# q and k of six head groups turned in 32x32 blocks on VectorE, with permuted products, in a routed attention and gated convolution kernel

## The chip, the core and the metric

The kernel runs on one core of one Trainium2 chip. A core has TensorE (PE: matmuls, and transposes done as matmuls against an identity), VectorE (DVE), ScalarE (ACT), GpSimd (POOL) and SyncE (SP, which here only issues DMAs). The metric is device time in microseconds of one execution; a profile is one further execution with the hardware profiler on.

## The reference, cut to what matters

```python
# q, k, v: [4, 8, 768, 64] f32; centroids: [8, 16, 64]
q_assign = argmax(q_n @ c_n^T)              # nearest of 16 centroids, per query (q_n, c_n: normalised)
k_assign = argmax(k_n @ c_n^T)              # the same per key
scores = where(q_assign == k_assign, (q @ k^T) / 8, -1e9)
attn = exp(scores - max(scores)); attn = attn / (sum(attn) + 1e-9)
x = attn @ v                                # heads side by side: [4, 768, 512]

proj = x @ w_proj                           # [.., 1536] -> x1, x2, x3 of 512
y = x1 * irfft(rfft(x2) * rfft(filter)) * x3     # circular convolution along the 768 rows
out = y @ w_out                             # [4, 768, 512] f32
```

## The kernel before

The 32 heads (4 batches of 8) are worked in eight *groups* of four heads, n = 0 to 7, and each group in two *pairs* of heads, pr = 0 and 1. Two groups make a batch. For each group the steps are:

- **Loads** (`load_qk`, `load_v`, on SP's queue). A q or k tile `qkraw` holds a pair's 768 rows as 128 partitions x 6 rows x 2 heads x 64 numbers; there are four such buffers (`NQK`), so all are used once per group. Each tile comes in two DMAs, one per head, with rows of 64 f32 (256 bytes). v (`vraw`, three buffers) comes in one DMA per pair.
- **Turning q and k** (`routing`). The scores need q and k with the 64 head dimensions on the partitions. For groups 2 to 7, `tr2` (line 594) makes 12 TensorE transposes of 128x128 per pair into three PSUM banks, six of q and six of k; three copies (the helper `copy`, lines 282 and 284) bring them by ACT or DVE to `qkP` in SBUF. Groups 0 and 1 use single banks (line 607).
- **Routing masks** (`routing`, continued). Centroid products by TensorE (line 627), a 32x32 block transpose of the result on DVE (line 632), a maximum, a comparison (lines 638, 640), a second block transpose (line 642), and eight small DMAs (line 497) put the one-hot rows under q and k in the `aug` tiles, where a large constant makes a mask of them. The `aug` tiles take q and k as bf16 casts from `qkP` (by ACT, DVE or POOL).
- **Attention** (`attention`). For each of six key tiles: scores by TensorE (helper `product`, line 84), exponentials by ACT (lines 694, 697) into one of five f32 buffers `p`, the product with v on TensorE in f32 (line 708), and the row sums, accumulated element by element in `acc`: the first two tiles are added in three 512-wide pieces (line 725, DVE or POOL), the other four in one 1536-wide addition each (line 729, DVE). After the sixth tile, ACT copies the result from PSUM to `osb` (line 732). `acc` is reduced across partitions by accumulating DMAs issued on POOL (line 762) and small DMAs on SP, or, in the first two groups and the last, by a matmul; the reciprocals are spread to `rb` (two DMAs to 64 partitions), and one DVE instruction (line 808) computes `(osb + eps) * rb` into the bf16 tile `xT`. `eps` is a column that the v product yields beside its 768 results.
- **Gated convolution** (`hyena`), once per batch: projections of `xT` (line 843), spectrum, product with the filter (line 873), inverse (line 84), folds (lines 944, 954), gates `x1 * x3` (line 917), the product with them (line 959), and the output projection.

The order of the work is not written by hand: every step is an operation with a duration, a set of engines that may run it, and a due time; a planner (`Plan.place`) puts them on the engines one by one, and the program is issued in that order. The tables `NUDGE` (a correction to the due time of each operation, by its number) and `ONLY` (a fixed engine for some) go into it. Each engine then runs its instructions in its order, and waits on semaphores where data or a buffer is not ready. Operations marked `lock` are those with SBUF operands on DVE and POOL; a POOL one of them is made to wait for the last DVE one ahead of it.

Of the kernel before, what the change touches and what calls it, by code (L numbers as in the profile page):

```python
# [18 lines left out]
Act = mybir.ActivationFunctionType  # L19
# [13 lines left out]
NV = 3  # L33
NU = 4
ROWS = 16
LEAD = 0.0
# [228 lines left out]
def build(T):  # L265
# [31 lines left out]
    def two(h):  # L297
        return T.pair[2]
# [16 lines left out]
    def load_qk(n, pr, j, due, after=()):  # L315
        s = qslot[n, pr, j] = len(loads) % NQK
        loads.append(1)

        src = lambda: (T.q, T.k)[j][n // 2, 4 * (n % 2) + 2 * pr:4 * (n % 2) + 2 * pr + 2].rearrange("h (p t) d -> p t h d", t=NT)
        for x in range(2):  # L320
            for half in ((0,), (1,)) if n == pr == 0 else ((0, 1),):
                t = slice(3 * half[0], 3 * half[-1] + 3)
                op({"SP": .66, "ACT": .66} if n == 0 else ("SP", .66), lambda e, x=x, t=t: dma(e)(
                    T.qkraw[s][:, t, x], src()[:, t, x]), due, w=[("qkraw", s, x, c) for c in half],
                   byts=98e3 * len(half), kind="load", after=after, lat=.3 if n else -.5)

    def load_v(n, pr, due, after=()):
        op(("SP", .6), lambda e: T.nc.sync.dma_start(
            T.vraw[(2 * n + pr) % NV], T.v[n // 2, 4 * (n % 2) + 2 * pr:4 * (n % 2) + 2 * pr + 2].rearrange(
                "h (p t) d -> p h (t d)", t=NT)), due, w=[("vraw", (2 * n + pr) % NV)], byts=LOAD, kind="load",  # L330
           after=after)
# [242 lines left out]
    def routing(n):  # L574
# [5 lines left out]
        for u in range(8):  # L580
# [7 lines left out]
            if n > 1 and z % 2 == 0 and ch == 0:  # L588
                h = Bank(cls, 3)
                ss = [qslot[n, pr, x] for x in range(2)]  # L590

                def tr2(e, ss=ss, h=h):
                    for i in range(2 * NT):
                        T.nc.tensor.transpose(bank(h.ids[i // 4])[:, ts(i % 4, 128)], raw(ss[i // NT], i % NT), T.ident[:, ::-1] if 3 <= i < NT else T.ident)  # L594
                op(("PE", 1.42), tr2, due, r=[("qkraw", s, x, c) for s in ss for x in range(2) for c in range(2)] + ["ident"], w=[h], alloc=h)
                for c in range(3):
                    op(EV512, lambda e, pr=pr, c=c, h=h: copy(e, T.qkP[pr][:, ts(c, 512)], bank(h.ids[c])), due + 1.6,
                       r=[h], w=[("qkT", 2 * pr + x, y) for x, y in ((0, 0), (0, 1), (0, 2), (1, 0), (1, 1), (1, 2))[2 * c:2 * c + 2]],
                       free=[h])
            elif n < 2:  # L600
                h = Bank(cls)

                def tr(e, s=s, ch=ch, j=j, h=h):
                    if n == 0:
                        awake(h)
                    for t in range(3):
                        T.nc.tensor.transpose(ap(h)[:, ts(t, 128)], raw(s, 3 * ch + t), T.ident[:, ::-1] if ch > j else T.ident)  # L607
                op(("PE", .36 if n else .58), tr, due, r=[("qkraw", s, x, c) for x in range(2) for c in ((0, 1) if n else (ch,))] + ["ident"] + ["cold"] * (n == 0), w=[h], alloc=h)
                op(EV384 if n != 1 else {"ACT": .48}, lambda e, z=z, ch=ch, h=h: copy(e, T.qkT[z][:, ch], ap(h)[:, :384]),
                   due + .6, r=[h], w=qk(z, ch), free=[h])  # L610
# [52 lines left out]
    def attention(n, pr, sins):  # L663
# [8 lines left out]
        for sk in range(NT):  # L672
# [31 lines left out]
            def pv(e, sk=sk):  # L704
                o = two(ob)
                for ch in range(2):
                    for hp in range(2):
                        T.nc.tensor.matmul(o[64 * hp:64 * hp + 64, ch, :385],  # L708
                                           T.vraw[vs][:, hp, sk * D:(sk + 1) * D],
                                           T.p[slots[sk]][:, hp, 384 * ch:384 * ch + 385],  # L710
                                           start=(sk == 0), stop=(sk == NT - 1))
            op(("PE", 1.3), pv, due, r=[("p", slots[sk], u) for u in range(3)] + [("vraw", vs), "eps"] +
               ([ob] if sk else []), w=[ob], alloc=None if sk else ob, kind="pv")
            AK = [("acc", os, u) for u in range(3)]
            if sk == 1:
                for u in range(3):
                    def part(e, u=u):
                        T_ = lambda x: x.rearrange("p a b -> p (a b)")
# [8 lines left out]
            if sk > 1:  # L727
                def acc(e, sk=sk):
                    T.nc.vector.tensor_tensor(T.acc[os], T.p[slots[sk]][:, :, :S], T.acc[os], op=Alu.add)  # L729
                op(("DVE", 1.75), acc, due + .2 - 40 * (last and sk == NT - 1), r=PK(sk), w=AK, lock=True)  # L730
        te = A(i0 + NT) + 2.0 - 40.0 * last
        op(("ACT", .79), lambda e: T.nc.scalar.copy(T.osb[o3], two(ob)[:, :, :385]), te, r=[ob], w=[("osb", o3)],  # L732
           free=[ob])
        late = n == NG - 1 or n < FIRST
        if late:
# [548 lines left out]
```

## Time and profile before

| | |
|---|---|
| median of 2 runs | 371.69 us (371.18 to 372.21) |
| profiled execution | 370.64 us, span 368.9 us |
| instructions | 8653 |
| moved by DMA | 46.20 MB in 90405 packets, 78248 of them under 512 bytes |
| read from and written to HBM | 31.59 MB, 7.40 MB |

The span is the time from the first to the last instruction that the profile shows. An engine's busy time is the time in which at least one of its instructions runs. A group's row names the line, the engine, the operation, the tiles (out<-in), the shape and type, the count, then the busy time in all and the mean duration of one in nanoseconds, then the idle time of the engine just before them and what ended it. Matmuls overlap in the records, so a mean duration of a matmul is not its cost; the chain of waits shows what a batch of them takes.

### The profile page before, as it was taken

Reading aid. Unit: us, or ns where it says so; the run is one execution under the profiler, and the core shown is the slowest. Engines: PE = TensorE matmul, PEld = TensorE weight load, DVE = VectorE, ACT = ScalarE, POOL = GpSimd, SP = SyncE. Lnnn points to the kernel's source line nnn. Section 1 sums busy time; section 2 is a strip of 40 time slices with the busy share of each in tenths; the row PEclk is TensorE's granted clock in tenths of the full one; section 3 lists DMA queues with packets and bytes.
Section 4 is the critical chain, followed back from the end, with each engine's and each line's share of the span. In section 5 each row is a group of like instructions: output and inputs, shape, how many; then the busy total and the mean of one; then the engine's idle time right before and its main releaser. Section 6 shows DMA issues by size and latency. Waiting matters only on the chain.

```text
span 368.9 us, 8653 instructions
## 1 busy us (share of the span) xinstructions
PE 357.5 (97%) x3314; PEld 208.9 (57%) x3316; DVE 342.5 (93%) x478; ACT 263.6 (71%) x495; POOL 120.9 (33%) x162
## 2 busy tenths in 40 slices
PE   7899999999999999999999999999999999999985
PEld 4455544555856565565555555566555655566672
DVE  7999999896999899999999999998998999999994
ACT  7998978877986859769869765899584785433242
POOL 7730730422032752331530044352221334016610
PEclk9999999999999999999999999999999999999999
DMA  7986597484247768748556964667477750110124
GB/s 175 202 189 126 128 211 195 93 189 110 62 80 156 115 156 169 152 103 129 107 64 183 238 170 81 146 152 98 81 116 167 150 77 1 48 45 2 59 115 171
DMA packets 90405, 46.20 MB, mean 125 GB/s; under 512 B 78248, under 2 KB 84092, under 8 KB 90364
## 3 DMA queue, kind: packets, MB, share of 16 engines
q1 hardware_dynamic: 85500, 36.15, 40.5%
q0 software_dynamic: 2752, 8.98, 17.1%
q10 hardware_dynamic: 2112, 0.52, 0.6%
q8 instruction: 26, 0.43, 0.5%
q14 instruction: 15, 0.12, 0.1%
HBM read 31.59 MB, written 7.40 MB: 106 GB/s over the span
## 4 chain that ended last, share of the span: by engine, by line
PE 78%; DVE 11%; ACT 5%; issue 3%; DMA 1%; POOL 1%; SPq 0%; DVEq 0%; ACTq 0%; POOLq 0%
PE bank L84 33%; PE pair L708 28%; PE bank L843 5%; PE bank L594 5%; DVE acc L729 3%; PE bank L627 2%; ACT p L697 1%; PE bank L82 1%; DMA qkraw<-in_k_dram 1%; DVE qkP L284 1%; PE bank L475 1%; PE bank L742 1%; ACT p L694 1%; PE bank L607 1%; DVE ohT L655 1%
## 5 line engine op out<-in xcount | busy, mean ns | idle before, releaser
L708 PE MATMUL pair<-p,vraw 128*64 128x385 f32 x768 | 143.0, 489 | 0.1
L697 ACT ACTIVATE p<-bank 128x512 f32<-128x512 f32 x192 | 108.7, 606 | 23.5 <-PE bank L84 16.0
L729 DVE TENSOR_TENSOR acc<-p,acc 128x1536 f32<-128x1536 f32 x64 | 112.8, 1762 | 3.2 <-ACT p L694 0.5
L84 PE MATMUL bank<-aug,aug 80*64 80x512 bf16 (+3 forms) x736 | 81.9, 327 | 2.1 <-ACT p L697 0.9
L708 PEld LDWEIGHTS pair<-p,vraw 128*64 128x64 f32 x768 | 56.6, 136 | 43.8 <-issue 36.7
L84 PEld LDWEIGHTS <-aug 80*64 80x64 bf16 (+1 forms) x736 | 45.6, 109 | 41.0 <-issue 26.3
L694 ACT ACTIVATE p<-bank 128x512 f32<-128x512 f32 x96 | 57.4, 606 | 5.4 <-PE bank L84 3.6
L284 POOL CAST aug<-qkP 64x768 bf16<-64x768 f32 x29 | 25.9, 900 | 83.3 <-DVE acc L729 55.9
L762 POOL DMA_DIRECT2D acc<-acc x30 | 24.4, 824 | 69.8 <-DMA acc<-acc 37.4
L84 PE MATMUL bank<-xT,wpj 128*64 128x384 bf16 x504 | 47.2, 326 | 0.0
L84 PEld LDWEIGHTS <-wpj 128*64 128x64 bf16 x504 | 30.2, 110 | 14.1 <-issue 2.6
L282 ACT COPY qkP<-bank 128x512 f32<-128x512 f32 (+1 forms) x46 | 23.1, 559 | 15.9 <-PE bank L594 9.7
L84 PEld LDWEIGHTS <-y 128*64 128x64 bf16 x472 | 24.0, 110 | 13.2 <-issue 3.6
L725 POOL TENSOR_TENSOR acc<-p,p 128x512 f32<-128x512 f32 x15 | 19.3, 1297 | 32.3 <-DVE acc L729 10.4
L873 DVE TENSOR_TENSOR tm<-bank,hm 128x512 f32<-128x512 f32 x44 | 28.1, 681 | 1.9 <-POOL uv L862 0.8
L84 PE MATMUL bank<-wout,y 128*64 128x512 bf16 (+1 forms) x200 | 24.0, 371 | 1.1 <-DVE y L959 1.1
L282 ACT CAST aug<-qkP 64x768 bf16<-64x768 f32 x28 | 23.2, 830 | 1.0 <-DVE qkP L284 0.4
L843 PE MATMUL bank<-wpj,xT 128*64 128x512 bf16 x192 | 22.7, 379 | 0.4 <-ACT p L697 0.4
L725 DVE TENSOR_TENSOR acc<-p,p 128x512 f32<-128x512 f32 x33 | 21.6, 690 | 0.4 <-DMA dd<-acc 0.4
L877 POOL TENSOR_TENSOR y<-tm 128x512 bf16<-128x512 f32 x14 | 17.8, 1277 | 12.8 <-DVE tm L873 10.6
L732 ACT COPY osb<-pair 128x770 f32<-128x770 f32 x16 | 12.9, 806 | 10.8 <-PE pair L708 10.7
L594 PEld LDWEIGHTS bank<-ident,qkraw 128*128 128x128 f32 x144 | 15.6, 141 | 6.3 <-ACT p L694 2.4
(178 smaller groups left out, 435.7 us busy)
## 6 DMA issues: line engine op xcount, KB each, us to landing
vraw<-in_v_dram SPq DMA_DIRECT2D x16, 384.0 KB, 5.2
qkraw<-in_q_dram SPq DMA_DIRECT2D x30, 192.0 KB, 3.9
rb<-dr SPq DMA_DIRECT2D x30, 192.0 KB, 3.7
qkraw<-in_k_dram SPq DMA_DIRECT2D x28, 192.0 KB, 3.6
out_dram<-ob SPq DMA_DIRECT2D x9, 512.0 KB, 5.0
acc<-acc POOLq DMA_DIRECT2D x10, 384.0 KB, 4.8
acc<-acc POOLq DMA_DIRECT2D x10, 192.0 KB, 4.2
y<-in_moe_filter_fft_dram SPq DMA_DIRECT2D x4, 384.0 KB, 4.3
```

What stands on the lines that cost most here:

```text
L84: T.nc.tensor.matmul(out[64 * i:64 * i + 64], lhsT[:, 64 * i:64 * i + 64], rhs, start=start, stop=stop)
L282: T.nc.scalar.copy(out, in_)
L284: (T.nc.vector if e == "DVE" else T.nc.gpsimd).tensor_copy(out, in_)
L594: T.nc.tensor.transpose(bank(h.ids[i // 4])[:, ts(i % 4, 128)], raw(ss[i // NT], i % NT), T.ident[:, ::-1] if 3 <= i < NT else T.ident)
L694: T.nc.scalar.activation(o, ap(h).rearrange("p (a b) -> p a b", a=2), Act.Exp, scale=0.125)
L697: T.nc.scalar.activation(flat(s)[:, lo:lo + 512], ap(h), Act.Exp, scale=0.125)
L708: T.nc.tensor.matmul(o[64 * hp:64 * hp + 64, ch, :385], T.vraw[vs][:, hp, sk * D:(sk + 1) * D], T.p[slots[sk]][:, hp, 384 * ch:384 * ch + ...
L725: alu(e).tensor_tensor(o, x, y, op=Alu.add)
L729: T.nc.vector.tensor_tensor(T.acc[os], T.p[slots[sk]][:, :, :S], T.acc[os], op=Alu.add)
L762: op(("POOL", .8), lambda e, rows=rows: T.nc.gpsimd.dma_start(flat_()[:rows], flat_()[rows:2 * rows], accum_op=Alu.add), te, r=[], w=AK, b ...
L843: T.nc.tensor.matmul(ap(h)[64 * i:64 * i + 64], T.xT[xs][:, kt, c:c + 64], T.wpj[:, kt, DM:2 * DM], start=kt == 0, stop=kt == ND - 1)
L873: op(("DVE", .68), lambda e, i=i, cs=cs, r=r, h=h: T.nc.vector.tensor_tensor(T.tm[r][:, cs], ap(h), hmrow(i, (0, 2, 2, 3)[2 * r + cs]), op ...
```

## The change

A list `TURN` names the pairs of groups 2 to 7. For these:

- q and k are loaded so that DVE can turn them. Each head's 768 rows go to 32 partitions x 24 rows, its dimensions 0 to 31 to one quarter of the partitions and 32 to 63 to the next, so a tile takes four DMAs of 32 partitions, with runs of 32 f32 (128 bytes). One DVE instruction per tile, a block transpose of 128x768 f32 from SBUF to SBUF, writes `qkP` directly. The transposes on TensorE, their banks and their copies are gone for these groups.
- The rows of a head then stand in another order: key tile and query column no longer hold row p*6+t but are permuted within each tile. v is loaded in the matching order, in four DMAs of 32 partitions.
- The scaling that writes `xT` puts the rows back in order: two products per pair, one for each half of the columns, that read `osb` and `rb` with a step of 32 numbers. `eps` is no longer added there but by ACT, which copies the `eps` column to `osb` first and uses it as the bias of the copy of the rest. The two products may go to POOL.
- The 1536-wide additions into `acc` may go to POOL as well as to DVE, and some operations of the last batch too: for its first two column tiles the gate is first copied from PSUM by ACT or DVE and then multiplied from SBUF by DVE or POOL.
- `xT` has a key for each half, so a projection of one half of the rows waits for that half alone.
- `NUDGE` and `ONLY` have new values throughout, so the order of nearly everything differs.

```diff
+TURN = [(n, pr) for n in range(2, NG) for pr in range(2)]
-NUDGE = {...}
-ONLY = {...}
+NUDGE = {...}
+ONLY = {...}
...
-        for x in range(2):
+        for x in range(2) if (n, pr) in TURN else ():
+            for y in range(2):
+                op(("SP", .66), lambda e, x=x, y=y: dma(e)(
+                    T.qkraw[s][64 * x + 32 * y:64 * x + 32 * y + 32].rearrange("p t h d -> p (t h d)").rearrange("p (c d) -> p c d", d=32),
+                    (T.q, T.k)[j][n // 2, 4 * (n % 2) + 2 * pr + x].rearrange("(p c) d -> p c d", c=4 * NT)[:, :, 32 * y:32 * y + 32]), due,
+                   w=[("qkraw", s, x, y)], byts=190e3, kind="load", after=after, lat=1.0)
...
     def load_v(n, pr, due, after=()):
+        for x in range(4) if (n, pr) in TURN else ():
+            op(("SP", .6), lambda e, x=x: T.nc.sync.dma_start(
+                T.vraw[(2 * n + pr) % NV][32 * x:32 * x + 32], T.v[n // 2, 4 * (n % 2) + 2 * pr:4 * (n % 2) + 2 * pr + 2].rearrange(
+                    "h (i p t) d -> p i h (t d)", p=4, t=NT)[x]), due, w=[("vraw", (2 * n + pr) % NV, x)], byts=LOAD / 4, kind="load",
+               after=after, lat=1.0)
...
-            if n > 1 and z % 2 == 0 and ch == 0:
+            if (n, pr) in TURN:
+                if ch == 0:
+                    op(("DVE", .98), lambda e, s=s, z=z, j=j: V().transpose(
+                        T.qkP[z // 2][:, ts(j, S)], T.qkraw[s][:].rearrange("p t h d -> p (t h d)").rearrange("p (q t d) -> p t q d", q=4, d=32)),
+                       due, r=[("qkraw", s, h_, y) for h_ in range(2) for y in range(2)], w=qk(z, 0) + qk(z, 1), lock=True)
+            elif n > 1 and z % 2 == 0 and ch == 0:
...
-                    T.nc.vector.tensor_tensor(T.acc[os], T.p[slots[sk]][:, :, :S], T.acc[os], op=Alu.add)
-                op(("DVE", 1.75), acc, ...)
+                    alu(e).tensor_tensor(T.acc[os], T.p[slots[sk]][:, :, :S], T.acc[os], op=Alu.add)
+                op({"DVE": 1.75, "POOL": 3.75}, acc, ...)
...
+        def bring(e):
+            if (n, pr) not in TURN:
+                T.nc.scalar.copy(T.osb[o3], two(ob)[:, :, :385])
+            else:
+                T.nc.scalar.copy(T.osb[o3][:, 1, 384:385], two(ob)[:, 1, 384:385])
+                T.nc.scalar.activation(T.osb[o3][:, :, :384], two(ob)[:, :, :384], Act.Identity, bias=T.osb[o3][:, 1, 384:385])
...
+        for a_ in [slice(0, 2)] if not turned else [slice(0, 1), slice(1, 2)]:
+            def scaled(e, a_=a_):
+                den = lambda: ap(rk[a_.start])[:, :384].unsqueeze(1) if last else rbv()[:, a_]
+                o, x, y = xv()[:, a_], osv()[:, a_], den()
+                if turned:
+                    perm = lambda z: z[:, 0].rearrange("p (t b i) -> p t i b", t=3, b=4)
+                    x, y, o = perm(x), perm(y), o[:, 0].rearrange("p (t i b) -> p t i b", t=3, b=4)
+                    if a_.start:
+                        o = o[:, :, ::-1, ::-1]
+                    alu(e).tensor_tensor(o, x, y, op=Alu.mult)
+                else:
+                    T.nc.vector.scalar_tensor_tensor(o, x, eps(), y, op0=Alu.add, op1=Alu.mult)
...
+                    elif last and dt < 2:
+                        op(EV384, lambda e, ch=ch, dt=dt, h=h: copy(e, T.x3[dt][:, ch], ap(h)[:, :384]), due + .8,
+                           r=[h], w=[("x3", dt, ch)], free=[h])
+                        op({"DVE": .55, "POOL": 1.1}, lambda e, ch=ch, dt=dt, x3=x3: alu(e).tensor_tensor(
+                            x3()[:, ch], T.x3[dt][:, ch], x3()[:, ch], op=Alu.mult), due + 1.4,
+                           r=[("x3", dt, ch)], w=xkeys[ch], lock=True)
```

## The prediction

> **What bounds the kernel now.** I read the busy times first, then the chain of waits, then three stretches of the span.
>
> ```profile
> span 368.9 us, 8653 instructions
> PE 357.5 (97%) x3314; PEld 208.9 (57%) x3316; DVE 342.5 (93%) x478; ACT 263.6 (71%) x495; POOL 120.9 (33%) x162
> PE 78%; DVE 11%; ACT 5%; issue 3%; DMA 1%; POOL 1%; SPq 0%; DVEq 0%; ACTq 0%; POOLq 0%
> ```
>
> ```profile
> core 0: us, PE busy (x) PEld busy (x) DVE busy (x) ACT busy (x) POOL busy (x), PEclk, DMA share, GB/s
> 0.00:30.00 30.00, 26.36 (x205) 14.89 (x207) 26.00 (x56) 25.92 (x50) 16.32 (x59) 1.00 0.88 192
> 30.00:360.00 330.00, 326.48 (x3069) 191.98 (x3069) 313.05 (x416) 235.11 (x441) 104.55 (x103) 1.00 0.56 118
> 360.00:368.90 8.90, 4.63 (x44) 2.08 (x40) 3.46 (x8) 2.52 (x5) 0.00 (x0) 1.00 0.47 177
> ```
>
> TensorE (PE) bounds it: 78% of the chain, and between 30 and 360 us it is idle 3.5 us of 330. VectorE (DVE) is close behind: 16.9 us idle there. ScalarE (ACT) has 95 us to spare, GpSimd (POOL) 225. The granted clock is 1.00 throughout. So work taken from PE is worth only as much as DVE, which gets it, can bear. The profiled execution took 370.64 us, 1.74 more than its span; the median of the runs, 371.69, lies 1.05 above that.
>
> **TensorE: what goes.** Twelve batches of twelve transposes (L594) leave PE. These lines of the chain show one batch, the P·V product right behind it, and a P·V product elsewhere:
>
> ```profile
> 150.08 1.47 PE bank L594 x12
> 151.55 1.45 PE pair L708 x8
> ...
> 188.64 1.30 PE pair L708 x8
> ```
>
> A batch takes 1.47 us, and the step behind it 0.15 longer than elsewhere. 12 x 1.62 = 19.4 us, all on the chain. PE's need in the middle stretch falls from 326.5 to 307.1 us; by PE alone the span would fall to about 350.
>
> **VectorE: what comes and goes.** The changed program's instruction order, compared with the old one, gives the counts; the durations are these:
>
> ```profile
> L729 DVE TENSOR_TENSOR acc<-p,acc 128x1536 f32<-128x1536 f32 x64 | 112.8, 1762 | 3.2 <-ACT p L694 0.5 <-POOL aug L284 0.4
> L725 DVE TENSOR_TENSOR acc<-p,p 128x512 f32<-128x512 f32 x33 | 21.6, 690 | 0.4 <-DMA dd<-acc 0.4
> L808 DVE SCALAR_TENSOR_TENSOR xT<-osb,rb 128x768 bf16<-128x768 f32 x15 | 15.1, 1007 | 0.0
> L954 DVE TENSOR_TENSOR yy<-sd 128x384 f32<-128x384 f32 x20 | 10.5, 551 | 0.9 <-POOL y L959 0.7
> L632 DVE STREAM_TRANSPOSE sim<-bank 128x384 f32<-128x384 f32 x14 | 7.5, 563 | 0.9 <-PE bank L627 0.7
> L642 DVE STREAM_TRANSPOSE ohB<-oh 128x768 bf16<-128x768 bf16 x7 | 6.8, 977 | 0.2
> L959 DVE TENSOR_TENSOR y<-yy,x 128x768 bf16<-128x768 f32 x7 | 6.7, 953 | 0.1
> L284 DVE COPY qkP<-bank 128x512 f32<-128x512 f32 x6 | 3.9, 683 | 0.9 <-PE bank L594 0.9
> L284 DVE CAST aug<-qkP 64x768 bf16<-64x768 f32 x7 | 3.8, 537 | 0.1
> ...
> L1036 DVE TENSOR_SCALAR kp<-kp 64x1 f32<-64x1 f32 x1 | 0.2, 151 | 0.1
> ```
>
> A DVE instruction that waits for nothing starts before the last has ended, which the timeline shows: two products from 343.92 and the next at 344.84 are 0.46 each, not 0.55; an accumulation from 103.47 holds DVE until 105.14, 1.67 and not 1.75.
>
> ```profile
> 103.47 1.75 DVE L729 TENSOR_TENSOR acc<-p,acc 128x1536 f32<-128x1536 f32 x1
> 105.14 1.00 DVE L808 SCALAR_TENSOR_TENSOR xT<-osb,rb 128x768 bf16<-128x768 f32 x1
> ...
> 343.92 1.01 DVE L917 TENSOR_TENSOR qkP<-bank,qkP 128x384 f32<-128x384 f32 x2
> 344.84 1.28 DVE L873 TENSOR_TENSOR tm<-bank,hm 128x512 f32<-128x512 f32 x2
> ```
>
> So I price an instruction at its duration less 0.085 us.
> - 24 block transposes of 128x768 f32 from SBUF. No row shows that form. The bf16 row of the same size has 977 ns, and the f32 row from PSUM 563 ns for half of it, 1126 at twice. I take 977, to which the size is nearest: 24 x 0.89 = +21.4. Bounds: at 1126, +3.6; at the slope between the two rows without the fixed part (0.83 us), -3.6.
> - 6 of 64 accumulations (L729) go to POOL: -6 x 1.68 = -10.1. Five 512-wide first sums come back from it: +3.0.
> - 6 copies of the transposes' result out of PSUM go: -3.6.
> - 11 of the 15 scalings of 768 (L808) go, each cut into two halves that are plain products, 14 on DVE and 8 on POOL: -10.1 + 14 x 0.47 = -3.6.
> - 3 gates of 768 (L959), 3 folds (L954) and 5 casts (L284) come: 2.6 + 1.4 + 2.3 = +6.3.
> - Of smaller instructions, most 384 wide, 13 go and 8 come, the last batch's gate products among them, which now go through a copy by ACT and partly POOL: -5 x 0.47 = -2.3.
>
> Sum: +11.1 us, with 26 instructions more: 313.1 + 11.1 = 324.2 us in the middle stretch, against 307.1 on PE. DVE becomes the bound.
>
> **The permuted reads.** The 14 products on DVE and the two at the very end read f32 with a step of 32 elements. The one strided read of the trace is L772's, with a step of 12:
>
> ```profile
> L638 DVE TENSOR_REDUCE mx<-sim 128x48 f32<-128x768 f32 x7 | 6.7, 950 | 0.2
> ...
> L772 DVE TENSOR_REDUCE dn<-dp 128x12 f32<-128x192 f32 x10 | 4.9, 487 | 0.0
> ...
> L529 DVE TENSOR_REDUCE mx<-bank 128x24 f32<-128x384 f32 x2 | 1.1, 546 | 0.0
> ```
>
> 768 elements take 950 ns and 384 take 546, 1.05 ns each, so 192 should take 344; the strided 192 take 487, 0.74 ns per element more. For 384 elements that is 0.28 us, for 16 products 4.5 us; the contiguous price is the other bound, 0. I take the middle, +2.2, since a reduction is not a product. The Trainium skill's page "SBUF — State Buffer" (§ Door 1: The DMA port swizzle) says the same against this change: f32 can be strided for free only up to four elements, since each access to a new 16-byte line pays. L772 agrees in sign; by the page's rule all of the 4.5 us would be due, and the sum 2.3 us longer.
>
> **How tightly DVE can run.** Count times mean over the 71 groups of DVE (first and last row above) is 368.2 us, against 342.5 busy: 25.7 us of overlap over 478 instructions, 0.054 each, where back-to-back ones overlap by 0.085. The rest had waited for another engine. A DVE that is late finds its inputs ready, so I take half of the difference: 442 instructions x 0.016 = -7.1 us (bounds 0 and -13.7). For idle time I give it what PE as the bound had in the middle, 3.5 us (bounds 2 and the 16.9 that DVE had). Start and end stay, 38.9 us: what is late there is the first loads and the last products and stores, and those are not taken away.
>
> The sum: 38.9 + 324.2 + 2.2 - 7.1 + 3.5 = 361.7 us of span, + 1.7 = 363.4: **363 us** as the profiled execution counts (the runs' median lay 1 us above it, which I leave to the range).
>
> **What is costed at nothing, and its cover.** ACT loses 30 copies and gets 12 small instructions (the offset column, copied ahead of the scaled copy of L732). POOL gets 6 accumulations:
>
> ```profile
> L697 ACT ACTIVATE p<-bank 128x512 f32<-128x512 f32 x192 | 108.7, 606 | 23.5 <-PE bank L84 16.0 <-PE pair L708 4.6 <-DVE acc L725 1.1
> L282 ACT COPY qkP<-bank 128x512 f32<-128x512 f32 x30 | 16.1, 594 | 10.1 <-PE bank L594 9.7 <-issue 0.5
> L725 POOL TENSOR_TENSOR acc<-p,p 128x512 f32<-128x512 f32 x15 | 19.3, 1297 | 32.3 <-DVE acc L729 10.4 <-DVE acc L725 9.1 <-ACT p L697 7.3
> ```
>
> ACT's 12, at 0.6 each at most, stay below the 17.8 it loses. A 1536-wide accumulation on POOL is about 3 x 1.30 = 3.9 us against 1.76: the next one of that head pair waits on DVE for it, with everything queued behind it, and a `p` buffer stays taken 2 us longer. POOL's 225 idle us cover the work, and DVE does other work meanwhile only as far as the order puts it there; without that cover, 6 x 2.1 = 13 us. The finer keys of `xT` (a projection waits for its own half of the rows alone) can only end waits earlier; I count nothing for them. POOL's waits on DVE lengthen, which nothing on the path sees.
>
> **The loads.** A q or k tile comes in four loads to 32 partitions instead of two to 128, and a v tile in four instead of one: 84 more issues on SP. The q and k loads stand in these rows (KB, time to landing; issue times of SP; time to landing, shortest, middle, longest):
>
> ```profile
> q1 hardware_dynamic: 85500, 36.15, 40.5%
> qkraw<-in_q_dram SPq DMA_DIRECT2D x30, 192.0 KB, 3.9
> rb<-dr SPq DMA_DIRECT2D x30, 192.0 KB, 3.7
> qkraw<-in_k_dram SPq DMA_DIRECT2D x4, 96.0 KB, 2.4
> ```
>
> ```profile
> L323 SPq DMA_DIRECT2D qkraw<-in_q_dram x33: 487/636/1952, 1.8 to 247.5; - x33
> DMA to landing us min/median/max: 2.4/3.8/6.9
> ```
>
> SP pays 84 x 0.64 = 54 us of issuing, of its own time. Each new load moves 96 KB in as many packets (768) as an old one of 192 KB, of 128 bytes: by bytes it lands in 2.4 us, by packets in 3.9. The 24 tiles have 36,864 packets more. Queue q1's 40.5% of 16 engines' 368.9 us over 85,500 packets is 28 ns each; at that, 64 us per DMA engine, 0.56 + 0.18 of the middle stretch, and less if a short packet is cheaper. The transfers fit, and a `qkraw` buffer is refilled once per head group, from one group's transposes to the next group's, so I cost them at nothing; the cover is that lead.
>
> **Rivals.**
> - *No gain* (0.18): DVE doesn't pack tighter, the strides cost in full, and it keeps 3.5 to 10 us of its idle time. 38.9 + 324.2 + 0 to 4.5 + 3.5 to 10 + 1.7 = 368 to 379. For it: its 16.9 us are many small waits, at nearly every form. Against: they are waits for PE, as in the rows of L632 and L284 above, and PE gets 16 us of slack.
> - *Slower, loads late* (0.12): DVE takes instructions in order, so a block transpose that stands at its turn before its fourth load has landed holds the accumulations behind it; these hold the `p` buffers, then the exponentials, then PE. In the old order PE did the transposes, and could be fed from a load that was late only with its own 1.5 us. The price is 24 times the wait: at 0.8 us, 363 + 19 = 382; it crosses the 2% border from (379 - 363)/24 = 0.7 us each. For it: landings range from 2.4 to 6.9 us, and the SP queue is in order too. Against: the lead above. The Trainium skill's page "SBUF — State Buffer" (§ Door 1: The DMA port swizzle) would make this likelier: a transfer to 32 partitions, like one to 64, reaches 8 of 16 ports, half the bandwidth. But `rb`, written 64 partitions at a time, lands 192 KB in 3.7 us, as fast as 128-partition `qkraw` in 3.9, so at this size the trace doesn't bear it out; by the rule the loads would land about 1.5 us later, and I leave it a third of this case.
> - *Slower, transposes dear* (0.06): f32 from SBUF at half rate, 24 x 0.9 = +21.6, 385 us. For it: no row has that form. Against: the f32 row from PSUM and the bf16 row cost the same per element.
> - *Better* (0.02): DVE packs wholly, 7 us less, 356 us or a little below.
>
> **Chances.** The forecast's own case has 0.62, spread evenly from 356 to 368 by the bounds of its terms. The borders of 2%, about what a measurement of this kernel can tell from no change, are at 364.3 and 379.1; of the 12 us 8.3 lie below the first: 0.43 faster, 0.19 the same. Faster 0.43 + 0.02 = 0.45; same 0.19 + 0.18 = 0.37; slower 0.12 + 0.06 = 0.18. The range 356 to 380 leaves out the slower cases and a few hundredths below.
>
> **What would show it.** DVE at 350 to 356 us busy, over 96% of the span, and most of the chain; PE near 338. Transposes near 0.98 us with no DMA as the releaser of their idle time; permuted products between 0.55 and 0.83. The forecast is wrong if DMA stands as a releaser ahead of the transposes for over 5 us in all, if DVE's idle time stays above 20, or if PE is still the bound.

## The result, and the profile after

| | before | after |
|---|---|---|
| median of 2 runs | 371.69 us (371.18 to 372.21) | 395.28 us (395.09 to 395.47) |
| span of the profiled execution | 368.9 us | 393.1 us |
| mean granted clock | 1.00 | 0.978 |

The ratio is 1.065 (95% interval 1.062 to 1.067): slower by 6.5%, where 363 us had been forecast. The page of the changed kernel begins with these lines (busy time and share of the span; the span in 40 slices; the chain of waits by engine and by line):

```profile
span 393.1 us, 8522 instructions
...
PE 355.5 (90%) x3198; PEld 202.3 (51%) x3198; DVE 360.8 (92%) x505; ACT 259.1 (66%) x488; POOL 129.1 (33%) x157
...
PE   7999999939999999898969989977969999989995
...
PEclk9999999987999999999989999998989999999999
...
PE 44%; DVE 26%; ACT 13%; issue 6%; SPq 6%; DMA 4%; ACTq 0%; POOL 0%; DVEq 0%; POOLq 0%
```

No engine is full. PE's row has holes that it did not have before, and the chain, which lay on PE for 78%, now changes engine all the time, a quarter of it on DVE. The busy time by stretches, cut as in the prediction:

```profile
core 0: us, PE busy (x) PEld busy (x) DVE busy (x) ACT busy (x) POOL busy (x), PEclk, DMA share, GB/s
0.00:30.00 30.00, 25.82 (x200) 14.53 (x202) 26.09 (x59) 25.50 (x48) 15.36 (x58) 1.00 0.79 179
30.00:384.20 354.20, 325.25 (x2957) 185.56 (x2955) 331.61 (x442) 230.30 (x435) 113.72 (x99) 0.98 0.59 111
384.20:393.10 8.90, 4.42 (x48) 2.18 (x42) 3.10 (x6) 3.28 (x7) 0.00 (x0) 1.00 0.47 177
```

Start and end are cut to the length that they had before, and hold about as much work as then (PE 25.8 and 4.4 us, before 26.4 and 4.6), so all of the difference lies between. The middle is 354.2 us: DVE works 331.6 of it and is idle 22.6, PE works 325.3 and is idle 28.9. The forecast had DVE at 319.3 there and idle 3.5. So of the 31.4 us by which the span (393.1) misses the forecast one (361.7), 12.3 are busy time of VectorE and 19.1 are idle time beside it.

The groups of the new operations:

```profile
L748 DVE TENSOR_TENSOR acc<-p,acc 128x1536 f32<-128x1536 f32 x58 | 103.7, 1787 | 5.9 <-POOL acc L748 2.7
...
L604 DVE STREAM_TRANSPOSE qkP<-qkraw 128x768 f32<-128x768 f32 x24 | 22.6, 959 | 0.0
L842 POOL TENSOR_TENSOR xT<-osb,rb 128x384 bf16<-128x384 f32 x8 | 12.1, 1523 | 28.4 <-DVE acc L748 16.9
```

The block transposes cost what was forecast, and DVE was never idle ahead of them. Next the waits of PE, and then those of DVE, the longest of each (who waited for whom: us in all, times, longest):

```profile
PE bank L85 <- DVE y L1000: 5.9, 4, 3.2
PE bank L767 <- DVE acc L748: 4.4, 2, 4.0
PE bank L85 <- ACT p L716: 3.9, 8, 1.0
PE bank L646 <- DVE qkP L604: 2.6, 1, 2.6
PE pair L727 <- ACT osb L756: 2.5, 4, 1.2
```

```profile
DVE acc L748 <- POOL acc L748: 2.7, 2, 2.4
DVE xT L842 <- DMA rb<-dr: 2.2, 2, 1.2
DVE sim L651 <- PE bank L646: 1.7, 1, 1.7
DVE sd L985 <- PE bank L85: 1.4, 1, 1.4
```

There is no single culprit: PE waits mostly for DVE, and DVE a little for everybody. The largest hole of PE shows how. Timelines of PE, then of DVE, around it (start, duration, what; in brackets the idle time before and its releaser):

```profile
79.39 1.46 PE L727 MATMUL pair<-p,vraw 128*64 128x385 f32 x8
84.85 0.85 PE L767 MATMUL bank<-acc,ones 128*32 128x384 f32 x8 [4.00 <-DVE acc L748]
88.32 2.79 PE L646 MATMUL bank<-qkP,cbd 128*32 128x384 f32 x16 [2.61 <-DVE qkP L604]
```

```profile
76.91 3.58 DVE L748 TENSOR_TENSOR acc<-p,acc 128x1536 f32<-128x1536 f32 x2
80.40 0.22 DVE L800 RECIPROCAL dn<-dn 128x12 f32<-128x12 f32 x1
80.66 0.56 DVE L674 TENSOR_SCALAR ohT<-bank 64x384 bf16<-64x384 f32 x1
81.25 3.55 DVE L748 TENSOR_TENSOR acc<-p,acc 128x1536 f32<-128x1536 f32 x2
84.72 3.55 DVE L604 STREAM_TRANSPOSE qkP<-qkraw 128x768 f32<-128x768 f32 x4
```

DVE works through 11 us without a pause, four accumulations with two short instructions between them and then four transposes, and PE, whose next two steps need just these, stands still for 4.0 and again for 2.6 us. The chain names SP's queue here, since a mask landed at the moment at which the accumulations ended:

```profile
83.08 1.66 DMA aug<-ohT
84.74 3.54 DVE qkP L604 x4
```

DVE had been busy all the while, so the chain doesn't decide between the two; a run below does.

### The profile page after: what moved, and what is told of

It reads as the page before. It is cut to its first block, busy times and chain, and to the rows that moved or that the text cites. A ratio compares the mean times of both kernels' runs of the same rounds, so it can differ in the third digit from the quotient of the medians.

```text
span 393.1 us, 8522 instructions
## 1 busy us (share of the span) xinstructions
PE 355.5 (90%) x3198; PEld 202.3 (51%) x3198; DVE 360.8 (92%) x505; ACT 259.1 (66%) x488; POOL 129.1 (33%) x157
## 3 DMA queue, kind: packets, MB, share of 16 engines
q1 hardware_dynamic: 123788, 35.86, 42.8%
## 4 chain that ended last, share of the span: by engine, by line
PE 44%; DVE 26%; ACT 13%; issue 6%; SPq 6%; DMA 4%; ACTq 0%; POOL 0%; DVEq 0%; POOLq 0%
PE bank L85 21%; PE pair L727 16%; DVE acc L748 5%; SPq L323 4%; ACT p L716 4%; PE bank L878 4%; DMA rb<-dr 3%; ACT aug L283 3%; DVE sd L985 2%; DVE yy L995 2%; DVE y L1000 2%; DVE qkP L604 2%; DVE tm L908 2%; ACT p L713 2%; DVE acc L744 1%
## 5 line engine op out<-in xcount | busy, mean ns | idle before, releaser
L748 DVE TENSOR_TENSOR acc<-p,acc 128x1536 f32<-128x1536 f32 x58 | 103.7, 1787 | 5.9 <-POOL acc L748 2.7
L85 PE MATMUL bank<-aug,aug 80*64 80x512 bf16 (+3 forms) x768 | 89.9, 334 | 9.3 <-ACT p L716 3.9
L85 PEld LDWEIGHTS <-aug 80*64 80x64 bf16 (+1 forms) x768 | 49.8, 111 | 54.2 <-issue 40.5
L85 PEld LDWEIGHTS <-wpj 128*64 128x64 bf16 x504 | 35.0, 110 | 14.5 <-issue 7.4
L283 ACT CAST aug<-qkP 64x768 bf16<-64x768 f32 x34 | 28.2, 830 | 12.1 <-DVE qkP L604 9.7
L285 POOL CAST aug<-qkP 64x768 bf16<-64x768 f32 x18 | 14.9, 830 | 50.9 <-DVE acc L744 15.4
L748 POOL TENSOR_TENSOR acc<-p,acc 128x1536 f32<-128x1536 f32 x6 | 20.7, 3452 | 21.2 <-ACT p L713 12.1
L283 ACT COPY x<-bank 128x384 f32<-128x384 f32 x24 | 11.1, 480 | 19.6 <-PE bank L85 14.0
L604 DVE STREAM_TRANSPOSE qkP<-qkraw 128x768 f32<-128x768 f32 x24 | 22.6, 959 | 0.0
L842 POOL TENSOR_TENSOR xT<-osb,rb 128x384 bf16<-128x384 f32 x8 | 12.1, 1523 | 28.4 <-DVE acc L748 16.9
```

What stands on the lines that cost most here:

```text
L85: T.nc.tensor.matmul(out[64 * i:64 * i + 64], lhsT[:, 64 * i:64 * i + 64], rhs, start=start, stop=stop)
L283: T.nc.scalar.copy(out, in_)
L604: op(("DVE", .98), lambda e, s=s, z=z, j=j: V().transpose(T.qkP[z // 2][:, ts(j, S)], T.qkraw[s][:].rearrange("p t h d -> p (t h d)").rear ...
L748: alu(e).tensor_tensor(T.acc[os], T.p[slots[sk]][:, :, :S], T.acc[os], op=Alu.add)
```

## The experiments

Three theories: **A**, VectorE simply has too much work; **B**, the loads, whose 84 further issues stand on SP's queue ahead of the small transfers that the path needs; **C**, the new order itself makes the engines wait for one another. Each median stands against runs of the kernel before on the same chip, whose medians were 370.75 to 371.16 us; brackets hold the 95% interval of the ratio. Differences from the changed kernel are taken from its 395.28 us, which was measured beside 371.69 us of the kernel before; the medians of the kernel before differ by up to 0.9 us, and such a difference is no surer than that.

### One cost taken away from the changed kernel, order kept

Products read without a step, so that the rows stay permuted:

```diff
-perm = lambda z: z[:, 0].rearrange("p (t b i) -> p t i b", t=3, b=4)
-x, y, o = perm(x), perm(y), o[:, 0].rearrange("p (t i b) -> p t i b", t=3, b=4)
+perm = lambda z: z[:, 0].rearrange("p (t b i) -> p t b i", t=3, b=4)
+x, y, o = perm(x), perm(y), o[:, 0].rearrange("p (t b i) -> p t b i", t=3, b=4)
```

> The changed kernel with the 24 scaling products reading and writing contiguously (rows of xT stay permuted, so the output rows are not put back in order); order and everything else as changed. Theory A (VectorE has too much work): VectorE's products go from 0.84 to 0.55 us, POOL's from 1.52 to about 1.0, VectorE busy falls by 4 to 5 us and the time by 4 to 8 us, to 387 to 391. Theory B (the loads: SP's queue and late data): no change, 394 to 396. Theory C (the new order itself, whose engines stall one another whatever single costs are): under 3 us.

391.85 us, 1.055 [1.049, 1.060]: 3.4 us less than the changed kernel. The same permutation, made by the write instead of the read:

```diff
-x, y, o = perm(x), perm(y), o[:, 0].rearrange("p (t i b) -> p t i b", t=3, b=4)
+x, y, o = perm(x), perm(y), o[:, 0].rearrange("p (t i b) -> p t b i", t=3, b=4)   # x, y contiguous
```

> The changed kernel with the products reading contiguously and permuting on the bf16 write instead; the result is the same. If the price is the strided f32 read, products fall to 0.55 us as in the run with contiguous products and the time with them; if a strided write costs as much as a strided read, they stay near 0.84 us and the time at 395.

392.78 us, 1.058 [1.054, 1.061]. The groups by form of the three kernels: the changed one, reads without a step, and steps on the write.

```profile
L842 DVE TENSOR_TENSOR xT<-osb,rb 128x384 bf16<-128x384 f32 x14 | 12.1, 873 | 2.2 <-DMA rb<-dr 2.2
L842 DVE TENSOR_TENSOR xT<-osb,bank 128x384 bf16<-128x384 f32 x2 | 1.6, 820 | 0.0
```

```profile
L842 DVE TENSOR_TENSOR xT<-osb,rb 128x384 bf16<-128x384 f32 x14 | 7.5, 546 | 5.4 <-DMA rb<-dr 5.4
...
L842 POOL TENSOR_TENSOR xT<-osb,rb 128x384 bf16<-128x384 f32 x8 | 7.9, 1000 | 29.0 <-DVE acc L748 17.3 <-DVE dn L798 5.4 <-ACT aug L283 5.3
```

```profile
L842 DVE TENSOR_TENSOR xT<-osb,rb 128x384 bf16<-128x384 f32 x14 | 13.6, 1003 | 1.8 <-DMA rb<-dr 1.8
...
L842 POOL TENSOR_TENSOR xT<-osb,rb 128x384 bf16<-128x384 f32 x8 | 8.3, 1063 | 29.2 <-DVE acc L748 17.4 <-ACT aug L283 5.5 <-DVE dn L798 5.1
```

A step of 32 f32 (128 bytes) on the reads costs VectorE 0.33 us a product and GpSimd 0.5. On the write the same permutation is a step of only 4 bf16 (8 bytes), and it costs VectorE 0.46 and GpSimd next to nothing. With the step on the write VectorE's products are dearer than in the changed kernel and only GpSimd's are cheaper, yet 2.5 of the 3.4 us are back; so the time fits the products on GpSimd better than those on VectorE. The two runs lie too close together (389.5 to 392.5 and 391.2 to 392.9 us) to settle it.

Half of each q and k load left out (dimensions 32 to 63) and v in one load in the old row order, so that SP issues as much, and the packets are as many, as before the change (the bytes of these q and k loads are halved too):

```diff
-op(("SP", .66), lambda e, x=x, y=y: dma(e)(...)
+op(("SP", .66), lambda e, x=x, y=y: y == 0 and dma(e)(...)
```

> The changed kernel with half of each q and k tile's load left out (dimensions 32 to 63 keep older data) and v of groups 2 to 7 in one DMA per pair, rows in the order of before: SP issues and packets of these loads as many as before the change. Theory B (loads): 10 us or more faster, 385 or less. Theories A and C: within 3 us of 395.

391.02 us, 1.054 [1.052, 1.056]: 4.3 us less. SP's queue has 0% of the chain now, and PE's timeline still has the hole shown above:

```profile
84.86 0.87 PE L771 MATMUL bank<-acc,ones 128*32 128x384 f32 x8 [4.01 <-DVE acc L752]
88.33 2.79 PE L650 MATMUL bank<-qkP,cbd 128*32 128x384 f32 x16 [2.60 <-DVE qkP L608]
```

So that hole was VectorE's: it is as long without the loads ahead of the mask.

The transposes narrowed to 32 columns; the rest of `qkP` stays what it was:

```diff
-T.qkP[z // 2][:, ts(j, S)], T.qkraw[s][:]...("p (q t d) -> p t q d", q=4, d=32)
+T.qkP[z // 2][:, S * j:S * j + 32], T.qkraw[s][:]...[:, :32]
```

> The changed kernel with each block transpose narrowed from 768 to 32 columns (five sixths and more of q and k of groups 2 to 7 keep older data): about 24 x 0.8 = 19 us of VectorE work left out, order and loads as changed. Theory A: 15 us or more faster, 380 or less. Theory B: within 3 us of 395. Theory C: some of it, 5 to 15 us.

393.0 us, 1.060 [1.056, 1.063]: VectorE's busy time is 17 us less, the time 2.3, and the interval overlaps that of the changed kernel (1.062 to 1.067) a little. PE's timeline at the same place:

```profile
84.03 0.85 PE L767 MATMUL bank<-acc,ones 128*32 128x384 f32 x8 [4.00 <-DVE acc L748]
...
91.83 2.83 PE L727 MATMUL pair<-p,vraw 128*64 128x385 f32 x8 [2.16 <-DMA vraw<-in_v_dram]
```

The wait of 2.6 us for the transposes is gone, and a little later PE waits 2.2 us for a load of v, which it did not do there in the changed kernel. So A as a plain count of work is wrong in this order, and one relief uncovers the next wait. All three together, products contiguous, loads halved and transposes narrowed:

> The changed kernel in its own order, with all three suspected costs taken away at once: products contiguous (rows stay permuted), half of each q and k load left out and v in one load, transposes narrowed to 32 columns. One at a time these gave back 3.4, 4.3 and 2.3 us of 395.3. If the costs add up and nothing else is new: 384 to 387 us. If each hides behind the others and the whole loss is theirs: 365 to 373 us. If the order itself, in which each engine's instructions are laid out, holds the loss: 380 us or more.

381.12 us, 1.031 [1.026, 1.036]: 14.2 us less, and still 10 us above the old kernel. The three singly add up to 10.0; the 4.2 us between are about as large as the scatter of the five medians allows, so whether the three costs hide one another stays open.

```profile
span 378.6 us, 8406 instructions
...
PE 350.7 (93%) x3198; PEld 197.8 (52%) x3198; DVE 336.0 (89%) x505; ACT 258.4 (68%) x488; POOL 124.6 (33%) x157
```

VectorE has less to do here than before the change (342.5), TensorE has its transposes gone, and both wait. One more part of the change, in the changed kernel with all its costs, the six sums on GpSimd:

```diff
-alu(e).tensor_tensor(T.acc[os], T.p[slots[sk]][:, :, :S], T.acc[os], op=Alu.add)
+T.nc.vector.tensor_tensor(T.acc[os], T.p[slots[sk]][:, :, :S], T.acc[os], op=Alu.add)
```

> The changed kernel with its six 1536-wide sums on GpSimd brought back to VectorE, order kept: VectorE 10.5 us more, GpSimd 20.7 less, the output the reference's. If GpSimd's slow sums (3.45 us each) hold the accumulations behind them: 390 to 394 us. If VectorE's amount of work is what counts: 398 to 406 us. If neither is near the path: 394 to 397 us.

409.18 us, 1.101 [1.095, 1.106]: 13.9 us more, above all that was expected. Taking 17 us from VectorE gave 2.3; giving it six sums more (some 10 us) cost 13.9. In this order the two directions are not alike. Part of the 13.9 may be TensorE's: its clock was 0.957 here against 0.978, and it was busy 7.6 us longer (363.1) with the same work.

### One cost put into the kernel before, order kept

The loads alone, for groups 2 to 7: q and k in four loads a tile with runs of 128 bytes, v in four loads of 32 partitions.

```diff
-dma(e)(T.qkraw[s][:, t, x], src()[:, t, x])
+[dma(e)(T.qkraw[s][:, t, x, d_], src()[:, t, x, d_]) for d_ in (slice(0, 32), slice(32, 64))]
```

> The kernel before, with each q and k load of groups 2 to 7 cut into two halves of the head dimension (runs of 128 bytes, four DMAs per tile) and v into four DMAs of 32 partitions: as many issues on SP and as many packets as the changed kernel, everything else as before. Theory B (loads): 8 us or more slower than before, 380 or more. Theories A (VectorE's work) and C (the order): within 3 us of 371.7.

389.96 us, 1.050 [1.044, 1.056]. No engine has other work than before, and 18.8 us are lost. The chain by engine; a piece of SP's timeline, and what VectorE did behind it; the longest waits of DVE:

```profile
PE 50%; SPq 14%; DMA 13%; DVE 12%; issue 6%; ACT 3%; POOL 0%; DVEq 0%; ACTq 0%; POOLq 0%
```

```profile
57.85 1.99 SPq L328 DMA_DIRECT2D vraw<-in_v_dram  x4
59.97 0.36 SPq L776 DMA_DIRECT2D dr<-dn  x1
60.37 1.25 SPq L323 DMA_DIRECT2D qkraw<-in_k_dram  x2
62.49 1.15 SPq L779 DMA_DIRECT2D rb<-dr  x2
...
67.63 1.02 DVE L808 SCALAR_TENSOR_TENSOR xT<-osb,rb 128x768 bf16<-128x768 f32 x1 [3.06 <-DMA rb<-dr]
```

```profile
DVE xT L808 <- DMA rb<-dr: 8.5, 4, 3.1
DVE acc L725 <- DMA dd<-acc: 4.9, 1, 4.9
```

Loads that are wanted later, here the four of a v tile, stand in the queue ahead of `dr`, the reciprocals on their way out; `rb`, the same reciprocals spread over the partitions, can only be issued when `dr` has landed; and VectorE's scaling waits 3.06 us for `rb`. VectorE now waits 13.4 us in all for `rb` and for the row sums; before the change its scaling waited for nothing (the row of L808 in the prediction has 0.0). The issues and the short runs apart; first the issues (loads of 64 partitions with runs of 256 bytes, v as above):

```diff
+[dma(e)(T.qkraw[s][r_, t, x], src()[r_, t, x]) for r_ in (slice(0, 64), slice(64, 128))]
```

> The kernel before, its order kept; for groups 2 to 7 each q or k load is cut into two loads of 64 partitions, and each v load into four of 32, so SP has 84 issues more as after the change, but the q and k runs stay 256 bytes and all packets stay as they were. Output is the reference's. The kernel with as many issues and short runs as well took 390 us against 371. If the number of issues on SP's queue is the cost: 384 to 391 us, with SPq among the first three of the chain. If the short runs (twice the packets) are the cost: 371 to 376 us.

380.0 us, 1.027 [1.023, 1.032]: 9.3 us, below the range expected. Then the runs alone, 128 bytes in as many loads as before:

```diff
+dma(e)(T.qkraw[s][:]...("p (c h d) -> p c h d", h=2, d=32)[:, :, x], src_)   # src_: 12 runs of 32 per partition
```

> The kernel before, its order kept; the q and k loads of groups 2 to 7 keep their number and their 128 partitions, but move runs of 128 bytes, so they have twice the packets (36,864 more). The halves of the two heads land side by side, so the scores are not the reference's. If the short runs are the cost: 383 to 391 us. If the issues on SP's queue are: 370 to 375 us. If both share it, both kernels lie near 380.

373.33 us, 1.008 [1.006, 1.010]: 2.6 us. Together they cost 18.8, apart 11.9. The durations of SP's DMA issues add up to 151 us before the change, 183 with short runs, 208 with more issues, 215 with both and 213 in the changed kernel. So the queue's busy time does not set the cost: alone the short runs add 32 us of issuing and cost 2.6 us, on top of the further issues they add 7 and cost 10. That it matters which transfer stands behind which fits the waits above, but was not tested by itself.

The permuted products alone, two per pair on VectorE, `eps` added by ACT, rows left permuted:

> The kernel before, with the scaling of groups 2 to 7 done as in the change but all on VectorE (two strided products per pair, eps added by ScalarE; rows of xT come out permuted): VectorE gets 24 x 0.76 less 11 x 0.92 and 2 x 0.52, about 7 us more, everything else and the order as before. Theory A: 3 to 8 us slower than before, 375 to 380. Theory B: no change. Theory C: 0 to 4 us, since the old order stays.

377.62 us, 1.017 [1.013, 1.020]: VectorE's busy time grew by 7.2 us (349.7), the time by 6.5.

The turn itself in the old order was built three times.

> The change's core in the old order: in the kernel before, the block transposes on VectorE stand where the first two of the three copies out of PSUM stood, the transposes on TensorE are gone, the loads come as in the change (v in two DMAs), products all on VectorE; no accumulation moves to POOL and NUDGE and ONLY are those of before. VectorE gets about 7 + 24 x 0.89 - 3.6 = 25 us more than before, 11 more than the changed kernel. Theory A: it is slower than the changed kernel, 395 to 405. Theory B: like the changed kernel, 390 to 400. Theory C (the new order is what loses): faster than the changed kernel in spite of more work on VectorE, 375 to 390.

436.45 us: the transposes stood at the place of the old copies, for some of the pairs behind the load that refills their buffer, so they turned the next group's data and waited for it (26.4 us in all). The time says nothing of the question.

> The kernel before in its old order, with the turn put into it: q and k loaded in quarters (four loads a tile), v in two loads, the block transposes on VectorE at the place where TensorE's transposes stood, permuted products, no TensorE transposes. Output is the reference's. If the new order is what costs (C): 368 to 380 us. If the loads on SP's queue do (B): 388 to 400 us, with SPq over 5% of the chain. If VectorE has too much work for any order (A): 380 to 390 us with VectorE over 96% busy.

418.95 us: here the transposes of both pairs wrote one `qkP` tile, so each waited for the other pair's readers, and the first pair's scores came from older data; not used either. Then with both mended:

```diff
+V().transpose(T.qkP[pr][:, ts(x, S)], T.qkraw[ss[x]][:]...("p (q t d) -> p t q d", q=4, d=32))  # x = 0, 1, at the first copy's place
```

> The kernel before in its old order with the whole turn in it: loads in quarters (four a tile), v in two loads, the 24 block transposes on VectorE at the place of the first copy of the old transposes, the loads that reuse a buffer issued behind them, two permuted products per pair. Output is the reference's. If the new order is what costs (C): 368 to 380 us. If the loads do (B): 388 to 400 us. If VectorE has too much work in any order (A): 380 to 395 us with VectorE over 95% busy.

420.68 us, 1.133 [1.126, 1.140]: the whole turn, in the order made for the old work, 50 us slower and above all that was expected. It is not the whole change: all sums and products stay on VectorE, v comes in two loads, and loads that reuse a buffer are issued later than before. Next the same with two loads a tile and one of v:

> As the kernel with the whole turn in the old order, but q and k in two loads a tile of 64 partitions (both heads' halves of the dimensions together) and v in one load in the old row order, so SP has as many issues as before; runs are still 128 bytes. The scores mix the halves of two heads. If SP's issues are the main cost (B): 12 to 20 us below the kernel with four loads a tile, 370 to 382 us. If VectorE's work is (A): within 5 us of it.

395.38 us, 1.066 [1.062, 1.069]. The 60 further issues make 25 us here (more than expected), and the rest 24.5. The chain by engine, of the turn with four loads a tile and of that with two:

```profile
PE 27%; DVE 26%; DMA 22%; SPq 11%; issue 7%; ACT 4%; POOL 1%; DVEq 0%; ACTq 0%; POOLq 0%
```

```profile
PE 38%; DVE 34%; issue 7%; DMA 7%; ACT 6%; SPq 5%; POOL 1%; DVEq 0%; ACTq 0%; POOLq 0%
```

C in its plain form, that the old order would carry the turn better, fails for the one way in which the turn was put into it: the new order, with the whole change in it, is 25 us better.

### Work taken away from the kernel before, order kept

What the change could gain in the old order: no turning at all for groups 2 to 7, neither transposes nor copies.

```diff
-T.nc.tensor.transpose(bank(h.ids[i // 4])[:, ts(i % 4, 128)], raw(ss[i // NT], i % NT), ...)
-copy(e, T.qkP[pr][:, ts(c, 512)], bank(h.ids[c]))
+pass
```

> The kernel before with the turning of q and k of groups 2 to 7 left out: no TensorE transposes, no copies of their result (the scores use what groups 0 and 1 left there); loads and order as they were. TensorE has 19 us less, VectorE and ScalarE their copies less. This is the ceiling of what the change could gain in the old order. If TensorE's removed work is worth its time there: 350 to 355 us. If VectorE, or the order itself, holds the span as soon as TensorE is lighter: 362 to 369 us.

368.18 us, 0.993 [0.991, 0.995]. What stood on the chain with 19.4 us gives 2.7 when it is simply gone. Is VectorE then the bound? Its own relief:

```diff
-T.nc.vector.tensor_tensor(T.acc[os], T.p[slots[sk]][:, :, :S], T.acc[os], op=Alu.add)
+T.nc.vector.tensor_tensor(T.acc[os][:, :, :32], ...)   # the fourth key tile of groups 2 to 7
```

> The kernel before, order kept, with VectorE made lighter instead of TensorE: in groups 2 to 7 the accumulation of the fourth key tile of each pair takes 32 columns only (12 of them, some 18 us of VectorE's time; the row sums miss the rest). If TensorE alone bounds the old kernel: 369 to 371 us. If VectorE alone does: 352 to 356 us. If the two hold each other in turn: 366 to 369 us, as little as TensorE's relief gave.

370.04 us, 0.998 [0.996, 1.000], with VectorE 17.5 us less busy (325.0). By itself that fits TensorE as the only bound; the 2.7 us of the run before exclude it. Neither, then, alone. Both:

> The kernel before, order kept, with both reliefs at once: the turning of q and k of groups 2 to 7 left out, and the 12 accumulations narrowed. If the two engines hold each other in turn: 350 to 358 us, much more than the 2.7 us of the one and what the other gives. If a third thing (the order's own waits, ScalarE, the small transfers) holds the span: 363 to 367 us, no more than the sum of the two.

362.27 us, 0.976 [0.974, 0.978]: 8.7 us, more than the 2.7 + 0.9 of the two, between the two ranges expected, and far from what the engines were relieved of (TensorE 16.4, VectorE 20.5).

```profile
span 361.4 us, 8321 instructions
...
PE 341.1 (94%) x3170; PEld 195.0 (54%) x3172; DVE 322.0 (89%) x472; ACT 249.0 (69%) x465; POOL 120.3 (33%) x162
...
PE 51%; DVE 22%; DMA 15%; issue 5%; ACT 4%; SPq 3%; POOL 0%; DVEq 0%; ACTq 0%
```

With both lighter, PE is idle 20 us and DVE 39, and DMA's share of the chain is 15%, where it was 1%; VectorE waits 6.5 us in all for `rb`, for which it did not wait before. So the transfers seem to come next, behind the two; no run made them lighter as well.

## Why the prediction was wrong, point by point

- **TensorE: what goes, "19.4 us, all on the chain".** This step failed first: the forecast took it as slack that would end VectorE's waits for PE. The amount was about right (PE's busy time is 16.4 us less in the run with both reliefs, 341.1 against 357.5), its worth was not: 2.7 us in the old order when nothing takes its place. A share of 78% of the chain said where the last wait was, not that the next one was far behind; VectorE, idle 16.9 us of 330 in the middle, was just behind. In the changed kernel PE's busy time is 355.5 and not near 338: the clock of 0.98 in the middle explains up to 7 us of it, the rest is not settled.
- **VectorE: what comes.** The terms were sized well: transposes 0.96 us against 0.98, and GpSimd's sums at 3.45 us against 3.9. The strided products were mis-sized: 14 at 0.87 and 2 at 0.82 us against 0.55 without the step, 14 x 0.33 + 2 x 0.27 = 5.1 us where I took 2.2 of 0 to 4.5. The Trainium skill's page "SBUF — State Buffer" (§ Door 1: The DMA port swizzle) says that each access to a new 16-byte line pays. For these reads the trace agrees: 0.87 against 0.55 us. The Trainium skill's page "GPSIMD Engine Reference" (§ 7. Performance pitfalls for Q7 kernels) gives half as much again for reads with a step over 8 bytes. The trace agrees: 1.52 against 1.00 us.
- **How tightly DVE can run, "-7.1" and "3.5 us" idle.** This failed with the largest sum, 19.1 + 7.1 of the 31.4 us. I gave VectorE the idle time that TensorE had had as the bound. It kept 22.6 us, in the many small waits shown above. Nor did its busy time pack: count times mean over its groups is 388.0 us against 360.8 busy, an overlap of 0.054 us for each of 505 instructions, as much as before the change. Busy time in the middle was 331.6, where 319.3 was forecast; of the 12.3 the packing that did not come explains 7.1, the strides 2.9, and 2.3 are not settled.
- **The loads, "I cost them at nothing".** The cover I named, the long lead of `qkraw`, held: no transpose waited for its load. What I didn't ask is who stands behind a load in SP's queue. The masks, the row sums' small steps and `rb` do, and they have no lead. In the old order that costs 18.8 us. In the changed kernel it is 4.3 alone, and perhaps a part of the 4.2 us by which the three costs together exceed their single sums. The transfers themselves were priced too high: queue q1's share went from 40.5% of 368.9 us to 42.8% of 393.1, 19 us per DMA engine where 64 was reckoned (and 64 of a middle stretch of 323 us would have been 0.20, not 0.18).
- **The rivals.** "Slower, loads late" had the right sign and the wrong mechanism: it waited for a DMA ahead of the transposes, and the row of L604 has 0.0 there. "Transposes dear" is excluded by the same row. "What would show it" worked: DVE idle for over 20 us was named as the sign of a wrong forecast, and it was 32.3 over the span. The products' 0.87 us, too, lies outside the 0.55 to 0.83 named.
- **GpSimd's sums.** Costed at nothing, with 13 us if the cover is gone. The cover held in the main: VectorE waited 2.7 us in all for such a sum (two waits, the longest 2.4), and bringing the six back to it cost 13.9 us.

What the runs show of the cause: what is put into the old order costs nearly in full or more (6.5 us for 7.2 of products, 18.8 for loads that give no engine more work), and what is taken from TensorE gives next to nothing there. The changed kernel pays for loads, strides and transposes (14 of its 24 us come back without them) with a relief that was worth some 3 us in the old order. The other 10 us stay open: why its order, with all three costs light, still takes 381 us, where the old order without any turning takes 368. There the new order is the worse one. That it was laid out around those costs is likely but was not shown, and no third order was tried.

## What to carry to other kernels

Before work is moved off the engine on the chain, leave it out and run that: the time it gives back is what the change can gain in that order, here 2.7 us of 19.4. Two engines that are both over 90% busy in a fixed order can hold each other: here relief on one alone showed little (2.7 and 0.9 us), relief on both 8.7, and load on VectorE nearly in full (6.5 of 7.2). Count what an added DMA delays behind it in its queue, not only whether its own data come in time.

## What the runs showed of the hardware

**The clock follows the holes.** Windows of 2 us of the changed kernel, from the end of the hole of 4.0 us on:

```profile
84.00:86.00 2.00, 0.85 (x8) 0.16 (x8) 2.00 (x3) 0.00 (x0) 0.00 (x0) 0.98 0.16 37
86.00:88.00 2.00, 0.00 (x0) 0.00 (x0) 2.00 (x3) 0.56 (x1) 0.00 (x0) 0.50 0.16 31
90.00:92.00 2.00, 2.00 (x16) 0.64 (x10) 0.82 (x2) 0.28 (x1) 0.00 (x0) 0.50 0.80 151
94.00:96.00 2.00, 2.00 (x20) 1.05 (x18) 1.98 (x4) 2.00 (x6) 0.00 (x0) 1.00 0.75 164
```

After the hole of 4.0 us the granted clock falls from 1.00 to 0.50, stays there through the hole of 2.6 us and the work behind it, and is back at 1.00 from 94 us on. The Trainium skill's page "TensorE: Matmul & The Clock Gate" (§ What's actually happening) says that an idle window of about 3.4 us halves the clock. The trace agrees. Over the span the mean of 0.978 is at most 8.6 us (0.022 x 393.1), so a long stall is paid twice: as idle time, and in slower matmuls behind it. I had taken the clock as 1.00, as it was before. Other kernels in which PE was idle longer than before (11.4 us of the span) had lower clocks too: 0.991 with the three costs light (27.9), 0.957 with the sums on VectorE (45.0), 0.963 with the turn in the old order (56.8). The idle time alone does not set it: with both reliefs it was 20.3 us, and the clock stayed at 1.00.

**Steps on the write.** A bf16 result written with a step of 4 elements (8 bytes) took VectorE 1.00 us for 384 columns, more than the f32 reads with a step of 32 (0.87) and nearly twice the contiguous form (0.55); on GpSimd this write was almost free (1.06 against 1.00).
